# Linear attention and an MLP mixer on one core: token mixing two slots sooner, and another order of phi, transposes and loads

## The chip, the core and the metric

The kernel runs on one core of one Trainium2 chip. The metric is the device time of one execution in microseconds (us); the time before is the median of three runs. Five engines work side by side and wait for one another by semaphores: PE (TensorE, matrix products), DVE (VectorE), ACT (ScalarE), POOL (GpSimd) and SP (SyncE, which here only issues DMAs). Each runs its own instructions strictly in the order in which the program gives them.

## What is computed

```
phi(x) = where(x > 0, x, exp(x) - 1) + 1
kv  = einsum('bhsd,bhse->bhde', phi(k), v);  z = sum_s phi(k)
x   = einsum('bhsd,bhde->bhse', phi(q), kv) / (einsum('bhsd,bhd->bhs', phi(q), z) + 1e-6)
x   = x.transpose(0, 2, 1, 3).reshape(8, 576, 512)
u   = x + (relu(x^T @ w_tok1) @ w_tok2)^T          # token mixing: 576 -> 256 -> 576
out = u + relu(u @ w_ch1) @ w_ch2                  # channel mixing: 512 -> 1536 -> 512
```

q, k and v are float32 of 8 batches, 8 heads, 576 rows and 64 columns; the output is float32. Products are made in bf16 and summed in float32.

## The kernel before, in words

**Tiles.** The 576 rows of a batch are 4 x 128 rows and a tail of 64; the tails of two batches share one tile of 128. `load` (L99) fetches one tensor of one batch for half of the heads with two DMAs of SP: 512 KB (L104) and the tail of 64 KB (L106). The raw tiles have two buffers per tensor, by even and odd batch, so the load of batch n + 2 waits until batch n's raw tile has been read.

**Steps of the attention of one batch.** `phi` makes phi(k) or phi(q) for half of the heads: an exponential on ACT (L116, "e"), then on DVE y = x + 1 (L122), a minimum (L130) and a maximum (L131, into "kp" or "qp"). `vcast` turns v into bf16 (L144 and the tail L145, into "vs" and "vst"). `kv` multiplies (L163) and ACT copies to "kvbd" (L167). phi(q) is transposed to "qT", for the first four batches by PE and a copy of ACT (`qtr`, L173 and L187), for later ones by one crossbar DMA of SP (`qtr_dma`, L191). `nd` makes numerator and denominator on PE (L200) and divides on DVE (L210 to L213, into "x").

**Token mixing.** `mm1` (L235) with a relu on ACT (L238, "ar"), then `mm2` (L246) for the row groups 0 and 1 ("mm2a"), 2 and 3 ("mm2b") and the tail ("mm2t"); DVE adds x and writes u (L252) or the tail's ut (L250). u is transposed to uT: for batches 0 and 1 by PE with copies (`utr`), for later ones by two crossbar DMAs of SP (`utr_dma`, L333); the tail goes to uTt (L338 from batch 3 on).

**Channel mixing.** `mm3` (L349) makes one of 12 blocks of 128 hidden channels from uT with four products of 128 x 512, and ACT applies the relu (L353, "cr"). `mm3_tail` (L360) does the same for the tails of a pair of batches. `mm4` (L372) multiplies by w_ch2 into one of nine output tiles of a pair; DVE adds u (L382, "o_sb"), and POOL (SP for the last pair) stores it. `mm3` and `mm4` share four PSUM banks, the small steps two tiles of two banks each.

**What sets the order.** `run` (L540) writes the order out by hand. The channel mixing of batch n is a row of slots: 12 of `mm3`; for odd n then 3 of `mm3_tail` and 15 of `mm4` (30 slots), for even n 12 of `mm4` (24 slots). Behind each slot come the small steps of the next batch that a table gives this slot number: `at0` in batch 0's loop, `at1` in batch 1's, `AT3` and `AT` later. One slot of four products keeps PE busy for 0.86 us. The phi and the casts of batch n + 2 and its loads stand in the same lists, so all engines' queues follow from these tables. In batch 0's loop, slots 12 to 23 are `m4_0`: one product for each of four output tiles at a time, which need all four banks of `mm3` free.

The DMAs of SP are issued in program order too: a load that waits holds up the transposes behind it, and the other way round. Batch 1's loads come first k, then v, then q; the second part of w_ch2 (POOL, L437) is made to wait for v's second half, and batch 2's first load for the third part of w_ch2.

The functions that the change touches, and what calls them:

Of the kernel before, what the change touches and what calls it, by code (L numbers as in the profile page):

```python
# [18 lines left out]
def kernel(  # L19
# [23 lines left out]
    R = 4  # L43
# [195 lines left out]

    def mm2(n, rs):  # L240
        b = n % 2
        m = len(rs)
        ps = ps_sm.tile([128, 2, DM], FP32, name="h_ps", tag="sm")
        for i, r in enumerate(rs):
            for kt in range(NT):
                nc.tensor.matmul(out=ps[:, i], lhsT=w2t[:, kt, b, :] if r == R else w2v[:, kt, r],  # L246
                                 rhs=ar[b][:, kt, :], start=(kt == 0), stop=(kt == NT - 1))
        if rs[0] == R:
            h = half[b]
            nc.vector.tensor_tensor(out=ut[n // 2 % 2][h], in0=ps[h, 0], in1=x[b][h, R], op=ALU.add)  # L250
        else:
            nc.vector.tensor_tensor(out=u[b][:, rs[0]:rs[0] + m], in0=ps[:, 0:m],  # L252
                                    in1=x[b][:, rs[0]:rs[0] + m], op=ALU.add)
# [173 lines left out]
    NB = 4  # L427
# [92 lines left out]
    def steps(n):  # L520
# [34 lines left out]
    def m4_0(kc):  # L555
        for t in range(R):
# [8 lines left out]
    fill += [(5, lambda: phi("k", 1, 0, HG)), (7, lambda: phi("k", 1, HG, HG)),
             (9, lambda: vcast(1, 0, nc.vector.tensor_copy)),
             (11, lambda: vcast(1, 1, nc.vector.tensor_copy))]
    fill += [(at0[nm], fn) for nm, fn in steps(1) if nm[:2] == "kv"]
    fill += [(12, lambda: phi("q", 1, 0, HG)), (12, lambda: phi("q", 1, HG, HG))]
    fill += [(at0[nm], fn) for nm, fn in steps(1) if nm[:2] in ("qt", "nd", "mm")]  # L570
    fill += [(23, lambda: mm4_end(0, 0))]
# [6 lines left out]
    big = m3(1) + m3t + m4(0, [4, 5, 6, 7, 8])  # L578
    at1 = {"kv0": 10, "kv1": 11, "qt0": 12, "qt1": 13, "nd00": 14, "nd01": 15, "nd10": 16,
           "nd11": 17, "nd20": 18, "nd21": 19, "mm1": 21, "mm2a": 23, "mm2b": 24, "mm2t": 26,  # L580
           "uta": 23, "utb": 24}
    fill = [(s, lambda g=g: prep_k(2, g, nc.vector.tensor_copy)) for g, s in ((0, 2), (1, 4))]
    fill += [(s, lambda g=g: phi("q", 2, HG * g, HG)) for g, s in ((0, 7), (1, 9))]
    fill += [(at1[nm], fn) for nm, fn in steps(2)]
    fill += [(s, lambda g=g: prep_k(3, g)) for g, s in ((0, 20), (1, 22))]
    fill += [(s, lambda g=g: phi("q", 3, HG * g, HG)) for g, s in ((0, 26), (1, 28))]
    fill += [(28, lambda: load_all(4, "qkv"))]
    run(big, sorted(fill, key=lambda e: e[0]))
    load_all(5, "qkv")

    AT3 = {"kv0": 0, "kv1": 1, "qt0": 2, "qt1": 3, "nd00": 4, "nd01": 5, "nd10": 6, "nd11": 7,
           "nd20": 8, "nd21": 9, "mm1": 11, "mm2a": 13, "mm2b": 14, "mm2t": 16, "uta": 13,
           "utb": 14, "utt": 16}
    AT = {"kv0": 0, "kv1": 1, "nd00": 3, "nd01": 4, "nd10": 5, "nd11": 6, "nd20": 7, "nd21": 8,
          "mm1": 10, "mm2a": 12, "mm2b": 13, "mm2t": 15, "uta": 12, "utb": 13, "utt": 15}
    for n in range(2, B):
        p, b = divmod(n, 2)
        if b == 0:
            big = m3(n) + m4(p, [0, 1, 2, 3])
        else:  # L600
            big = m3(n) + m3t + m4(p, [4, 5, 6, 7, 8] if n + 1 < B else [8, 4, 5, 6, 7])
# [41 lines left out]
```

## Time and profile before

| what | value |
|---|---|
| median of 3 runs (lowest to highest) | 287.98 us (287.26 to 289.92) |
| the profiled execution | 288.99 us |
| its span, first to last instruction | 287.2 us |
| PE busy | 264.2 us (92%) |
| DVE, ACT, POOL busy | 165.3, 145.9, 29.2 us |
| mean granted clock of PE | 0.992 |
| moved by DMA | 47.98 MB, mean 167 GB/s |

The profile is one execution. A row of a timeline has the start in us from the span's beginning, the duration (of several merged instructions, if it ends in x4 and the like), the engine, the line of the kernel, the operation, output and inputs, and in square brackets how long the engine stood idle before it and what ended this. A row with an engine's name and a "q" is the issue of a DMA, not its transfer. In the waits, a row gives who waited for whom, the total, how often, and the longest. In the table by stretches, each engine has its busy time and its count; the last three columns are PE's granted clock (1.00 is full), the mean busy share of the DMA engines and the GB/s that they moved.

### The profile page before, as it was taken

The page shows a single profiled execution, that of the slowest core. Times are in us where ns is not written, and L with a number is a line of the kernel's source. Part 1 is how long each engine was busy: PE and PEld are TensorE (multiplying, and loading weights), DVE is VectorE, ACT ScalarE, POOL GpSimd, SP SyncE. Part 2 cuts the span into 40 slices and gives each one's busy share as a digit, 9 for nine tenths or more (in the row PEclk, how much of TensorE's full clock was granted, in tenths as well). Part 3 has the DMA queues.
Part 4 walks back from the last instruction along what each step waited for, and adds up shares of the span by engine and source line. Part 5 has one row for each costly group of instructions (what it writes and reads, how often), then busy time and mean ns, then how long its engine had stood idle before and what let it go on. Part 6 is the DMA issues. An engine that isn't in the chain of part 4 may idle for free.

```text
span 287.2 us, 4625 instructions
## 1 busy us (share of the span) xinstructions
PE 264.2 (92%) x1784; PEld 146.8 (51%) x1804; DVE 165.3 (58%) x327; ACT 145.9 (51%) x233; POOL 29.2 (10%) x52
## 2 busy tenths in 40 slices
PE   8798978979999789897999999998999999999993
PEld 8776444544754345343556455444565454444641
DVE  4885276767877925767476718593858444520021
ACT  3664776038974337770677335943577065106400
POOL 3090020003000210002000220011000210000000
PEclk9999999999999979999999999999999999999999
DMA  6979999999701799999974994096009310340031
GB/s 209 280 109 198 281 271 177 290 282 341 220 21 52 129 276 311 289 229 267 288 211 92 252 351 150 2 192 138 2 0 189 123 37 0 69 137 34 2 110 73
DMA packets 70901, 47.98 MB, mean 167 GB/s; under 512 B 39328, under 2 KB 67872, under 8 KB 70880
## 3 DMA queue, kind: packets, MB, share of 16 engines
q1 hardware_dynamic: 64384, 36.84, 51.8%
q0 software_dynamic: 6496, 10.85, 15.7%
q8 instruction: 14, 0.23, 0.3%
q14 instruction: 7, 0.06, 0.1%
HBM read 35.85 MB, written 9.44 MB: 158 GB/s over the span
## 4 chain that ended last, share of the span: by engine, by line
PE 65%; DMA 14%; ACT 6%; SPq 5%; DVE 5%; issue 3%; POOL 1%; ACTq 0%
PE h_ps L372 25%; PE c_ps L349 23%; DMA uT<-u 6%; DMA q_raw<-in_q_dram 6%; PE a_ps L235 5%; PE h_ps L246 4%; DMA wc<-in_moe_w_ch_dram 3%; PE c_ps L360 3%; PE nd_ps L200 3%; SPq L106 3%; ACT e L116 2%; PE kv_ps L163 2%; SPq L104 2%; DVE u L252 1%; ACT cr L353 1%
## 5 line engine op out<-in xcount | busy, mean ns | idle before, releaser
L349 PE MATMUL c_ps<-uT,wc 128*128 128x512 bf16 x384 | 93.0, 382 | 7.1 <-DMA uT<-u 6.3
L353 ACT ACTIVATE cr<-c_ps 128x512 bf16<-128x512 f32 x96 | 56.3, 600 | 78.3 <-PE c_ps L349 78.3
L372 PE MATMUL h_ps<-wc,cr 128*128 128x512 bf16 x375 | 88.0, 379 | 0.8 <-DMA wc<-in_moe_w_ch_dram 0.3
L372 PEld LDWEIGHTS <-cr 128*128 128x128 bf16 x384 | 36.9, 98 | 41.6 <-issue 0.4
L349 PEld LDWEIGHTS <-wc 128*128 128x128 bf16 x384 | 35.8, 98 | 43.1 <-DMA uT<-u 5.8
L382 DVE TENSOR_TENSOR o_sb<-h_ps,u 128x512 f32<-128x512 f32 x32 | 21.5, 686 | 18.7 <-PE h_ps L372 18.7
L386 POOL DMA_DIRECT2D out_dram<-o_sb x24 | 14.4, 601 | 162.4 <-DVE o_sb L382 145.1
L213 DVE TENSOR_TENSOR x<-nd_ps,den 128x512 bf16<-128x512 f32 (+1 forms) x48 | 28.9, 603 | 1.7
L210 DVE TENSOR_SCALAR den<-nd_ps 128x8 f32<-128x8 f32 (+1 forms) x48 | 7.8, 162 | 33.7 <-PE nd_ps L200 33.2
L130 DVE TENSOR_SCALAR e<-e 128x1280 bf16<-128x1280 bf16 (+1 forms) x34 | 16.0, 471 | 14.7 <-ACT e L116 14.7
L252 DVE TENSOR_TENSOR u<-h_ps,x 128x1024 bf16<-128x1024 f32 x14 | 16.6, 1219 | 12.5 <-PE h_ps L246 12.5
L116 ACT ACTIVATE e<-k_raw 128x1280 bf16<-128x1280 f32 x16 | 20.4, 1273 | 4.2 <-DMA k_raw<-in_k_dram 4.1
L116 ACT ACTIVATE e<-q_raw 128x1280 bf16<-128x1280 f32 (+1 forms) x18 | 20.5, 1156 | 2.7 <-DMA q_raw<-in_q_dram 1.9
L200 PEld LDWEIGHTS <-qT 128*128 128x128 bf16 x160 | 12.6, 98 | 11.3 <-ACT qT L187 0.7
L200 PE MATMUL nd_ps<-kvbd,qT 128*128 128x130 bf16 x160 | 16.8, 221 | 0.7 <-ACT kvbd L167 0.5
L238 ACT ACTIVATE ar<-a_ps 128x512 bf16<-128x512 f32 x14 | 7.6, 594 | 19.2 <-PE a_ps L235 19.2
L122 DVE TENSOR_SCALAR y<-k_raw 128x1280 bf16<-128x1280 f32 x16 | 13.1, 821 | 4.7 <-DMA k_raw<-in_k_dram 4.5
L405 PE MATMUL bank<-identity 128*128 128x128 bf16 x178 | 13.6, 244 | 1.4 <-POOL identity masks.py:199 1.4
L246 PE MATMUL h_ps<-ar,w 128*128 128x512 bf16 x53 | 14.2, 379 | 0.2
L235 PE MATMUL a_ps<-x,w 128*128 128x512 bf16 x50 | 14.1, 379 | 0.3
L122 DVE TENSOR_SCALAR y<-q_raw 128x1280 bf16<-128x1280 f32 x16 | 13.2, 825 | 1.8 <-DMA q_raw<-in_q_dram 1.5
L131 DVE TENSOR_TENSOR qp<-e,y 128x1280 bf16<-128x1280 bf16 (+1 forms) x18 | 13.5, 752 | 0.6
(86 smaller groups left out, 238.2 us busy)
## 6 DMA issues: line engine op xcount, KB each, us to landing
k_raw<-in_k_dram SPq DMA_DIRECT2D x16, 512.0 KB, 7.5
q_raw<-in_q_dram SPq DMA_DIRECT2D x16, 512.0 KB, 7.4
v_raw<-in_v_dram SPq DMA_DIRECT2D x16, 512.0 KB, 8.1
out_dram<-o_sb POOLq DMA_DIRECT2D x24, 256.0 KB, 4.3
wc<-in_moe_w_ch_dram POOLq DMA_DIRECT2D x8, 384.0 KB, 8.2
out_dram<-o_sb SPq DMA_DIRECT2D x8, 256.0 KB, 2.5
k_raw<-in_k_dram SPq DMA_DIRECT2D x16, 64.0 KB, 7.1
q_raw<-in_q_dram SPq DMA_DIRECT2D x16, 64.0 KB, 6.9
```

Source lines behind the costliest of these rows:

```text
L116: nc.scalar.activation(out=e, in_=f, func=AF.Exp)
L122: nc.vector.tensor_scalar(out=y, in0=f, scalar1=1.0, scalar2=None, op0=ALU.add)
L130: nc.vector.tensor_scalar(out=e, in0=e, scalar1=1.0, scalar2=None, op0=ALU.min)
L200: nc.tensor.matmul(out=ps[:, i, a * 2 * D1:(a + 1) * 2 * D1], lhsT=qT[b][:, r, j, :], rhs=kvbd[b][:, j, :], start=True, stop=True)
L213: nc.vector.tensor_tensor(out=x[b][:, rs[0]:rs[0] + m, HG * D * g:HG * D * (g + 1)].rearrange("p r (h d) -> p r h d", h=HG), in0=v_[:, :, ...
L235: nc.tensor.matmul(out=ps[:, mt], lhsT=w1t[:, b, ms] if r == R else w1[:, r, ms], rhs=x[b][:, r, :], start=(r == 0), stop=(r == R))
L246: nc.tensor.matmul(out=ps[:, i], lhsT=w2t[:, kt, b, :] if r == R else w2v[:, kt, r], rhs=ar[b][:, kt, :], start=(kt == 0), stop=(kt == NT ...
L252: nc.vector.tensor_tensor(out=u[b][:, rs[0]:rs[0] + m], in0=ps[:, 0:m], in1=x[b][:, rs[0]:rs[0] + m], op=ALU.add)
L349: nc.tensor.matmul(out=ps, lhsT=wc1[:, kj, 128 * mc:128 * mc + 128], rhs=uT[b][:, :, kj], start=(kj == 0), stop=(kj == NDM - 1))
L353: nc.scalar.activation(out=cr[b][:, mc, :], in_=ps, func=AF.Relu)
L372: nc.tensor.matmul(out=ps, lhsT=crt[:, kc, :] if t == 8 else cr[b][:, kc, 128 * r:128 * r + 128], rhs=wc2[:, kc, :], start=(kc == 0), stop ...
L382: nc.vector.tensor_tensor(out=o, in0=ps, in1=ut[p % 2] if t == 8 else u[b][:, r, :], op=ALU.add)
```

## The change

- In batch 0's loop the loads of batch 1 come in the order k, q, v, and the second part of w_ch2 waits for q's second half. phi q goes to slots 9 and 11, its transposes to 12 and 13, and v's casts and both kv products behind them to 14 (before: casts 9 and 11, kv 11, phi q 12, transposes 14 and 15). nd and mm1 move one slot forward, mm1 from 22 to 21; mm2 stays at 23.
- For batch 1 alone `mm2` of the row groups 2 and 3 adds x on PE, by two more products with the identity, and ACT copies the result to u; for the row groups 0 and 1 DVE adds as before.
- In batch 1's loop phi k of batch 2 moves from slots 2 and 4 to 0 and 2, without v's casts, which come at 4 (now on ACT) and 5 (DVE); phi q from 7 and 9 to 6 and 8; kv from 10 and 11 to 7 and 8; the transposes, nd and mm1 one slot forward (mm1 from 21 to 20), mm2a and mm2b and the transposes of u from 23 and 24 to 21 and 22, the tail from 26 to 24. phi k and the casts of batch 3 go from 20 and 22 to 19 and 23, phi q from 26 and 28 to 25 and 27. Batches 4 and 5 are loaded at slots 24, 25 and 28, in the order k, v, q, where batch 4 was loaded at slot 28 and batch 5 behind the loop, each q, k, v.
- From batch 2's loop on nd, mm1, mm2 and the transposes of u stand one slot sooner, both kv products in slot 0. phi q of batch n + 2 moves from slots 9 and 11 to 8 and 9 (9 and 10 in batch 2's loop), phi k with the casts from 17 and 19 to 14 and 16 (15 and 17). qT's crossbar transpose goes from slot 11, ahead of u's, to slot 12 (13), behind u's. The loads of batch n + 4 come together at slot 18 (before: q at 15, k and v at 20).

The diff, cut to its core (the tables' rows are told above):

```diff
-    def mm2(n, rs):
+    def mm2(n, rs, add=False):
...
                 nc.tensor.matmul(out=ps[:, i], lhsT=w2t[:, kt, b, :] if r == R else w2v[:, kt, r],
-                                 rhs=ar[b][:, kt, :], start=(kt == 0), stop=(kt == NT - 1))
+                                 rhs=ar[b][:, kt, :], start=(kt == 0),
+                                 stop=(kt == NT - 1 and not add))
+            if add:
+                nc.tensor.matmul(out=ps[:, i], lhsT=identity, rhs=x[b][:, r, :], start=False,
+                                 stop=True)
...
+        elif add:
+            nc.scalar.copy(out=u[b][:, rs[0]:rs[0] + m], in_=ps[:, 0:m])
...
     for g in range(2):
+        landed["q1", g] = load("q", 1, g)
+    for g in range(2):
         landed["v1", g] = load("v", 1, g)
-    for g in range(2):
-        landed["q1", g] = load("q", 1, g)
-    c2_in += [after(load_wc2(i), landed["v1", 1] if i == 1 else None) for i in range(1, NB)]
+    c2_in += [after(load_wc2(i), landed["q1", 1] if i == 1 else None) for i in range(1, NB)]
...
-                 ("mm2b", lambda: mm2(n, [2, 3])), ("mm2t", lambda: mm2(n, [R]))]
+                 ("mm2b", lambda: mm2(n, [2, 3], n == 1)), ("mm2t", lambda: mm2(n, [R]))]
...
-           "uta": 23, "utb": 24}
-    fill = [(s, lambda g=g: prep_k(2, g, nc.vector.tensor_copy)) for g, s in ((0, 2), (1, 4))]
+           "uta": 21, "utb": 22}
+    fill = [(s, lambda g=g: phi("k", 2, HG * g, HG)) for g, s in ((0, 0), (1, 2))]
+    fill += [(4, lambda: vcast(2, 0)), (5, lambda: vcast(2, 1, nc.vector.tensor_copy))]
...
-            fill += [(15, lambda: load_all(n + 4, "q"))]
-            for g, s in ((0, 17), (1, 19)):
-                fill += [(s, lambda g=g: prep_k(n + 2, g))]
-            fill += [(20, lambda: load_all(n + 4, "kv"))]
+            d = 1 if n == 2 else 0
+            fill += [(s + d, lambda g=g: phi("q", n + 2, HG * g, HG)) for g, s in ((0, 8), (1, 9))]
+            fill += [(12 + d, lambda: qtr_dma(n + 2))]
+            fill += [(s + d, lambda g=g: prep_k(n + 2, g)) for g, s in ((0, 14), (1, 16))]
+            fill += [(18, lambda: load_all(n + 4, "kvq"))]
```

Three places show what this does to the order of an engine. The lines of the changed kernel are seven higher from `mm2` on (L252 becomes L259). The number behind a name is its buffer: k_raw_78, q_raw_82, x_93 and u_97 belong to odd batches, k_raw_77, q_raw_81, x_92 and u_96 to even ones. A row may stand for several instructions (x2).

ACT in batch 0's loop, from the eighth block of `mm3` on. Before:

```order
L353 ACTIVATE cr_103<-c_ps 128x512 x2
L116 ACTIVATE e<-k_raw_78 128x1280
L353 ACTIVATE cr_103<-c_ps 128x512 x4
L167 CAST kvbd_91<-kv_ps 64x2x65 x4
L116 ACTIVATE e<-q_raw_82 128x1280 x2
L187 COPY qT_89<-tp 128x2x5x128 x2
L238 ACTIVATE ar_95<-a_ps 128x512 x2
```

Now:

```order
L360 ACTIVATE cr_103<-c_ps 128x512 x2
L116 ACTIVATE e<-k_raw_78 128x1280
L360 ACTIVATE cr_103<-c_ps 128x512 x2
L116 ACTIVATE e<-q_raw_82 128x1280
L360 ACTIVATE cr_103<-c_ps 128x512 x2
L116 ACTIVATE e<-q_raw_82 128x1280
L187 COPY qT_89<-tp 128x2x5x128 x2
L167 CAST kvbd_91<-kv_ps 64x2x65 x4
L238 ACTIVATE ar_95<-a_ps 128x512 x2
```

The first exponential of phi q has moved ahead of the last two relus, and the copies of kv behind those of qT.

DVE in batch 1's loop, behind the last x of batch 2. Before:

```order
L382 TENSOR_TENSOR o_sb<-h_ps,u_97 128x512
L122 TENSOR_SCALAR y<-k_raw_78 128x1280
L130 TENSOR_SCALAR e<-e 128x1280
L131 TENSOR_TENSOR kp<-e,y 128x4x5x64
L122 TENSOR_SCALAR y<-k_raw_78 128x1280
L130 TENSOR_SCALAR e<-e 128x1280
L131 TENSOR_TENSOR kp<-e,y 128x4x5x64
L382 TENSOR_TENSOR o_sb<-h_ps,u_97 128x512
L252 TENSOR_TENSOR u_96<-h_ps,x_92 128x1024 x2
```

Now:

```order
L122 TENSOR_SCALAR y<-k_raw_78 128x1280
L130 TENSOR_SCALAR e<-e 128x1280
L131 TENSOR_TENSOR kp<-e,y 128x4x5x64
L389 TENSOR_TENSOR o_sb<-h_ps,u_97 128x512
L259 TENSOR_TENSOR u_96<-h_ps,x_92 128x1024 x2
L389 TENSOR_TENSOR o_sb<-h_ps,u_97 128x512
L122 TENSOR_SCALAR y<-k_raw_78 128x1280
L130 TENSOR_SCALAR e<-e 128x1280
L131 TENSOR_TENSOR kp<-e,y 128x4x5x64
```

Both writes of u stand between the halves of phi k now, where they stood behind both.

SP at the end of the burst of loads, in batch 2's loop. Before:

```order
L104 DMA v_raw_80<-in_v_dram 128x4x256
L106 DMA v_raw_80<-in_v_dram 64x4x64
L191 DMA_TRANSPOSE qT_88<-qp 128x20x128
L333 DMA_TRANSPOSE uT_101<-u_97 128x8x128 x2
L104 DMA q_raw_81<-in_q_dram 128x4x256
```

Now:

```order
L104 DMA q_raw_82<-in_q_dram 128x4x256
L106 DMA q_raw_82<-in_q_dram 64x4x64
L340 DMA_TRANSPOSE uT_101<-u_97 128x8x128 x2
L191 DMA_TRANSPOSE qT_88<-qp 128x20x128
L345 DMA_TRANSPOSE uTt<-ut_99 128x4x128
L104 DMA k_raw_77<-in_k_dram 128x4x256
```

u's transposes stand directly behind the loads and ahead of q's, and all three transposes ahead of batch 6's first load.

More of the change, by code (lines that the diff above doesn't have):

```diff
@@ L560 @@
         [lambda kc=kc: m4_0(kc) for kc in range(NCH)]
-    at0 = {"kv0": 11, "kv1": 11, "qt0": 14, "qt1": 15, "nd00": 16, "nd01": 17, "nd10": 18,
-           "nd11": 19, "nd20": 20, "nd21": 21, "mm1": 22, "mm2a": 23, "mm2b": 23, "mm2t": 23,
+    at0 = {"qt0": 12, "qt1": 13, "kv0": 14, "kv1": 14, "nd00": 15, "nd01": 16, "nd10": 17,
+           "nd11": 18, "nd20": 19, "nd21": 20, "mm1": 21, "mm2a": 23, "mm2b": 23, "mm2t": 23,
            "ut": 23, "utt": 23}
@@ L565 @@
     fill += [(5, lambda: phi("k", 1, 0, HG)), (7, lambda: phi("k", 1, HG, HG)),
[L566 to L570, printed above, removed]
+             (9, lambda: phi("q", 1, 0, HG)), (11, lambda: phi("q", 1, HG, HG))]
+    fill += [(14, lambda g=g: vcast(1, g, nc.vector.tensor_copy)) for g in range(2)]
+    fill += [(at0[nm], fn) for nm, fn in steps(1) if nm[:2] in ("kv", "qt", "nd", "mm")]
     fill += [(23, lambda: mm4_end(0, 0))]
@@ L602 @@
         fill = []
-        if n + 2 < B:
-            fill += [(s, lambda g=g: phi("q", n + 2, HG * g, HG)) for g, s in ((0, 9), (1, 11))]
-            fill += [(11, lambda: qtr_dma(n + 2))]
         if n + 1 < B:
```

24 lines of the change are left out of this document (12 added, 12 removed).

## The prediction

> **What bounds the kernel now.** I read the busy shares first, then TensorE's waits, its timeline at each wait, and there the timelines of the engine or queue that ended the wait.
>
> ```profile
> PE 264.2 (92%) x1784; PEld 146.8 (51%) x1804; DVE 165.3 (58%) x327; ACT 145.9 (51%) x233; POOL 29.2 (10%) x52
> PE c_ps L349 <- DMA uT<-u: 6.3, 3, 3.2
> ```
>
> TensorE (PE) is the bound: 264.2 of 287.2 us. So a change can only take the 23 us in which PE stands, or the stretch in which it runs at a lower clock. The longest wait of the big loops is for uT, the crossbar transpose of u (6.3 us in 3 waits). Here are these waits in PE's timeline, with one that DVE ends, and then rows of the table by stretches of time.
>
> ```profile
> 101.93 1.89 PE L349 MATMUL c_ps<-uT,wc 128*128 128x512 bf16 x4 [3.19 <-DMA uT<-u]
> 106.46 1.03 PE L349 MATMUL c_ps<-uT,wc 128*128 128x512 bf16 x4
> 119.66 0.38 PE L235 MATMUL a_ps<-x,w1t 128*128 128x512 bf16 x1 [1.27 <-DVE x L213]
> 135.33 1.02 PE L349 MATMUL c_ps<-uT,wc 128*128 128x512 bf16 x4 [1.70 <-DMA uT<-u]
> 138.19 1.89 PE L349 MATMUL c_ps<-uT,wc 128*128 128x512 bf16 x8
> 196.78 1.02 PE L349 MATMUL c_ps<-uT,wc 128*128 128x512 bf16 x4 [1.37 <-DMA uT<-u]
> ...
> 102.00:104.00 2.00, 2.00 (x8) 0.90 (x9) 0.32 (x1) 0.09 (x1) 1.07 (x2) 0.50 0.98 297
> 104.00:106.00 2.00, 2.00 (x15) 1.30 (x13) 0.00 (x0) 1.03 (x3) 0.00 (x0) 0.66 0.97 275
> 133.00:136.00 3.00, 1.30 (x7) 0.44 (x6) 1.50 (x3) 0.00 (x0) 1.08 (x2) 1.00 1.15 248
> ```
>
> The reader is to see two prices of one wait. After the 3.19 us the granted clock is 0.50 and then 0.66 (third column from the right); after the 1.70 us it stays 1.00. Two channel steps with both kv products take 138.19 - 135.33 = 2.86 us at full clock, but 106.46 - 101.93 = 4.53 us behind the long wait: 1.67 us more. The wait at 101.93 thus costs 4.86 us. With 1.27, 1.70 and 1.37 that is 9.2 us behind us 98.
>
> Durations come from one execution of 288.99 us (span 287.2, so 1.79 lies around it), 1.01 above the median of 287.98. I take the sum off the median.
>
> **Part by part. Batch 1's loop (us 64 to 102).** The mixing of batch 2 moves two slots forward, and the second half of phi k of batch 3 goes behind u. From the timelines of DVE, PE, ACT and SP:
>
> ```profile
> 92.18 0.49 DVE L130 TENSOR_SCALAR e<-e 128x1280 bf16<-128x1280 bf16 x1 [1.80 <-ACT e L116]
> 94.05 2.35 DVE L252 TENSOR_TENSOR u<-h_ps,x 128x1024 bf16<-128x1024 f32 x2
> ...
> 92.96 1.03 PE L246 MATMUL h_ps<-ar,w 128*128 128x512 bf16 x4
> ...
> 89.77 1.09 ACT L238 ACTIVATE ar<-a_ps 128x512 bf16<-128x512 f32 x2 [5.66 <-PE a_ps L235]
> 95.98 2.75 PE L372 MATMUL h_ps<-wc,crt 128*128 128x512 bf16 x12
> ...
> 95.30 3.64 SPq L333 DMA_TRANSPOSE uT<-u  x2
> 99.03 1.34 SPq L104 DMA_DIRECT2D q_raw<-in_q_dram  x1
> ```
>
> Before, DVE stood 1.80 us for phi k's exponential and only then made u, ending at 96.40; the batch's products end at about 98.73 and uT is there 5.53 us after u. After: a slot is four products, 0.86 us, so the second product ends at 93.99 - 1.73 = 92.27. Only one slot now lies between mm1 and mm2, less than the 1.09 us of ar, so PE waits some 0.35 us: 92.6. With 0.2 us to start and 1.22 for the last u (row of 2.35 for two) u ends at 94.0, 2.4 us sooner. PE ends at 99.1, uT is there at 99.5.
>
> But ACT gets more to do early in this loop: the cast of v's first half moves to it from DVE, and the exponentials come sooner, ahead of cr tiles. From ACT's timeline, and PE's one wait for it:
>
> ```profile
> 82.59 1.08 ACT L144 CAST vs<-v_raw 128x1024 bf16<-128x1024 f32 x1
> 83.70 0.41 ACT L145 CAST vst<-v_raw 64x256 bf16<-64x256 f32 x1
> 67.16 0.60 ACT L353 ACTIVATE cr<-c_ps 128x512 bf16<-128x512 f32 x1 [0.27 <-PE c_ps L349]
> 78.25 1.22 ACT L187 COPY qT<-tp 128x1280 bf16<-128x1280 bf16 x1
> ...
> 81.14 0.40 PE L200 MATMUL nd_ps<-kvbd,qT 128*128 128x130 bf16 x4 [0.23 <-ACT qT L187]
> ```
>
> 1.08 + 0.41 come to about 1.35 us overlapped. ACT was nearly full from 65 to 81; of its gaps there (the 0.27 shown and two like it just before) 0.8 us can be used up. Walking the new order with these durations, kv0 waits for the cast, the second q transposes for phi, and nd for both qT copies: about 1.4 us of PE waits for 0.23 before and some slots won; I take 0.75 us lost, between 0 (kv comes three slots sooner and gives slack) and 2.0 (all of the cast and of a delayed exponential). PE and u slip together, so the stage gains 101.93 - 99.5 - 0.75 = 1.7, and 1.9 with a little from the transposes, whose first now runs 1.7 us ahead of the second. The remaining wait of about 0.4 is far under 3.19, so the 1.67 us of slow clock go too. **Sum 3.6.**
>
> **Batch 2's loop.** phi q of batch 4 stood on DVE ahead of the last x; that is where 1.27 came from. Now both halves stand behind all x and ahead of u: **1.27 gained**, and u is delayed by phi for 1.3 us, which the rest of the loop covers. At the loop's end the SP queue counts (its timeline, with the rows of DVE and PE that it is measured against):
>
> ```profile
> 120.73 1.13 SPq L106 DMA_DIRECT2D v_raw<-in_v_dram  x1
> 121.97 6.73 SPq L191 DMA_TRANSPOSE qT<-qp  x1
> 128.80 2.81 SPq L333 DMA_TRANSPOSE uT<-u  x2
> ...
> 153.65 2.95 SPq L191 DMA_TRANSPOSE qT<-qp  x1
> ...
> 125.48 1.22 DVE L252 TENSOR_TENSOR u<-h_ps,x 128x1024 bf16<-128x1024 f32 x1
> ...
> 127.42 6.21 PE L372 MATMUL h_ps<-wc,cr 128*128 128x512 bf16 x27
> ...
> DMA to landing us min/median/max: 3.0/4.5/5.8
> ```
>
> u was there at 126.7, yet uT was issued at 128.80 behind qT, which itself stood 6.73 us behind the burst of loads (2.95 where none are ahead). Now uT stands in front of qT: 2.95 sooner; and the loads begin when batch 2's u is through, 1.65 sooner (2.4 - 0.75): 124.2. The last row (uT's DMAs) gives 3.0 to 5.8 to landing; I take 5.3, in its upper half, since loads are still ahead: 129.5. PE arrives after 28.76 us of loop (127.42 + 6.21 - 101.93, less 1.67 and 1.27) behind a start at 100.0: 128.8. A wait of 0.7 stays of 1.70: **1.0 gained** (0 to 1.7). Behind uT waits qT now, some 3 us later, 132.5; nd of the next loop wants it after three slots and the kv products, 129.5 + 2.6 + 1.1 = 133.2: just hidden, and each us that uT is later beyond that is paid by PE.
>
> The Trainium skill, "DMA: Bandwidth & Descriptors", Queues, rings and completion order, says that a DMA engine takes one queue's descriptors in ring order. That speaks against the change: a burst issued at once must drain before uT. The 6.73 us agree.
>
> **Batch 4's loop.** No loads are in the way there:
>
> ```profile
> 186.10 2.35 DVE L252 TENSOR_TENSOR u<-h_ps,x 128x1024 bf16<-128x1024 f32 x2
> 186.24 3.11 SPq L191 DMA_TRANSPOSE qT<-qp  x1
> 189.45 3.55 SPq L333 DMA_TRANSPOSE uT<-u  x2
> ```
>
> With qT's 3.11 behind it, uT lands some 3 us sooner and PE would have needed only 1.37: **1.37 gained**. The loops of batches 3 and 5 (30 slots) wait for nothing now; their gain is nothing. That k, v and q are loaded together at slot 18 costs nothing: they are used a loop later, some 30 us, and stand behind every transpose of their own loop. Nor do both kv products in slot 0: kp and vs are made in the loop before.
>
> **Batch 0's loop (us 26 to 64).** q lands where v did, so phi q fills the time before kv. From the timelines again:
>
> ```profile
> 38.05 2.06 ACT L353 ACTIVATE cr<-c_ps 128x512 bf16<-128x512 f32 x4
> 40.21 0.40 PE L163 MATMUL kv_ps<-vs,kp 128*128 128x130 bf16 x4 [1.36 <-DVE vs L144]
> 45.80 0.73 PE L173 MATMUL tp<-identity,qp 128*128 128x128 bf16 x10 [1.06 <-DVE qp L131]
> 46.85 1.02 PE L372 MATMUL h_ps<-wc,cr 128*128 128x512 bf16 x4 [0.32 <-DMA wc<-in_moe_w_ch_dram]
> 43.09 1.27 ACT L116 ACTIVATE e<-q_raw 128x1280 bf16<-128x1280 f32 x1 [0.35 <-DMA q_raw<-in_q_dram]
> 41.09 2.24 POOL L437 DMA_DIRECT2D wc<-in_moe_w_ch_dram  x3 [19.39 <-DMA v_raw<-in_v_dram]
> 58.71 2.14 PE L246 MATMUL h_ps<-ar,w 128*128 128x512 bf16 x7
> 60.03 2.35 DVE L252 TENSOR_TENSOR u<-h_ps,x 128x1024 bf16<-128x1024 f32 x2 [4.17 <-PE h_ps L246]
> ```
>
> Waits of 1.36 and 1.06 seem to be the prize, but most return: an exponential of 1.27 now stands ahead of two cr, so the four banks that the output products need are free at 41.4 rather than 40.1; and wc2's second part still lands at 46.85, as its gate is the load in the same place. By then PE has done one more set of transposes than before: 0.57 us. mm1 a slot sooner takes away 0.4 of waiting for ar (58.71 took 2.14 for 1.73 of products). u's second half goes to ACT beside DVE, 1.2 us side by side, for two more products of 0.43 and the ACT copy's longer chain: 0.2. **Sum 1.1** (-1 to 1.8).
>
> Total: 1.1 + 1.9 + 1.67 + 1.27 + 1.0 + 1.37 = 8.3 us; 287.98 - 8.3 = **279.7 us**.
>
> **Rivals.** *ACT sets batch 1's loop* (2.0 lost instead of 0.75), uT of batch 2 comes 0.5 later and the 1.0 at batch 2's end is not won: 279.7 + 1.25 + 0.5 + 1.0 = 282.5. For it: the full ACT rows; against it: kv's three slots of slack.
>
> *The median run has no slow clock to lose.* The runs of before lie at 287.26 to 289.92, the profiled one 1.01 above the median; if the median run does not pay the 1.67, they cannot be won: 281.4. For it: that spread is as wide as the price. Against it: the wait of 3.19 comes from the order, which is the same in every run. The Trainium skill, "TensorE: Matmul & The Clock Gate", Part 1, bears on this: the clock falls after an idle window of about 3.4 us whose start runs freely, so a wait of 3.19 would meet it in some runs alone; the trace shows one run, in which it fell.
>
> *uT is no sooner*, the change not doing what it says: DMA takes what u won, since loads follow directly. Then 3.6 falls to -0.75 and 1.0 to 0: 1.1 + 1.27 + 1.37 - 0.75 = 3.0, 285.0. Against it: loads stand behind uT in the queue.
>
> *q late in batch 0's loop*: if q lands at 43.09 as now, ACT stops at its exponential with two cr behind it and PE starts its output products at 45.4 instead of 41.7, with a wait long enough for the slow clock: 279.7 + 3.7 + 1.7 = 285.1. Against it: v1, in that place, had landed by 41.09 (POOL's row).
>
> *The burst holds uT of batch 3*: slower. Twelve pairs of loads stand ahead of it; their sizes and the rates of two stretches:
>
> ```profile
> k_raw<-in_k_dram SPq DMA_DIRECT2D x16, 512.0 KB, 7.5
> k_raw<-in_k_dram SPq DMA_DIRECT2D x16, 64.0 KB, 7.1
> 98.00:102.00 4.00, 0.81 (x5) 0.20 (x4) 3.90 (x7) 0.00 (x0) 0.44 (x1) 0.99 0.84 188
> 124.00:126.00 2.00, 2.00 (x11) 1.00 (x10) 2.00 (x3) 2.00 (x4) 0.14 (x1) 1.00 1.14 287
> ```
>
> 7.1 MB from us 98: at the 287 GB/s of most of the burst they end at 123, at the 188 of the stretch beside transposes at 135.6. uT would land 4.5 later (the median above), 11.3 us after PE's arrival and with the slow clock again: 287.98 - 7.3 won elsewhere + (11.3 - 1.7) + 1.7 = 292.0. The change is slower from a wait of 7.3 us on, that is with the burst under about 210 GB/s. Against it: the burst has 275 at us 104 and 287 at 124.
>
> **How the numbers follow.** Forecast 0.55 (own range 277.2 to 281.7: batch 1's loss 0 to 2.0, batch 0's gain -1 to 1.8, batch 2's 0 to 1.7, not all at one end), no slow clock 0.13, ACT 0.15, uT no sooner 0.06, q late 0.06, burst 0.05. The range of 277.0 to 284.3 takes in the first three and leaves out the last three. One per cent, 2.9 us, is about what a measurement here can tell from no change: faster (under 285.1) takes the first three and, as they end at 285.0 and 285.1, half of the next two, 0.89 and a little less for what I do not see: 0.88; same 0.07; slower 0.05.
>
> **What would show it.** PE's wait before batch 2's first channel product under 1 us and no granted clock under 0.9 behind us 90; no wait for x in batch 2's loop; uT ahead of qT and under 1 us of waiting at the ends of batches 2 and 4; in batch 0's loop output products from about 41.4. I am wrong if PE's waits between 70 and 82 pass 2 us, or uT's wait moves to batch 2's end and grows.

## The result, and the profile after

| | before | after |
|---|---|---|
| median of 4 runs each (lowest to highest) | 288.52 us (287.26 to 289.92) | 279.2 us (278.03 to 279.61) |
| ratio, 95% interval | | 0.967 (0.961 to 0.973) |
| profiled execution, span | 288.99 us, 287.2 us | 279.19 us, 277.4 us |

The change makes the kernel 3.3% faster; 279.7 had been predicted. Disturbed runs are left out of the ratios but not of the medians below, and the profiled executions of experiments 1 and 4 are such runs, 3.1 and 2.8 us above their kernels' medians, so I read their waits for their place and not for their size.

First the busy times of the changed kernel, then from its timeline of PE the first product of the channel mixing of batches 1 to 5, each the start of that batch's loop:

```profile
PE 262.3 (95%) x1786; PEld 146.3 (53%) x1806; DVE 164.6 (59%) x324; ACT 147.6 (53%) x236; POOL 28.6 (10%) x52
```

```profile
63.15 3.19 PE L356 MATMUL c_ps<-uT,wc 128*128 128x512 bf16 x14
98.40 1.03 PE L356 MATMUL c_ps<-uT,wc 128*128 128x512 bf16 x4
126.84 1.03 PE L356 MATMUL c_ps<-uT,wc 128*128 128x512 bf16 x4
159.64 1.03 PE L356 MATMUL c_ps<-uT,wc 128*128 128x512 bf16 x4
186.97 1.03 PE L356 MATMUL c_ps<-uT,wc 128*128 128x512 bf16 x4
```

None of these rows has a bracket: PE no longer waits for uT at any of them. PE does 1.9 us less of busy time with two products more, which fits the end of the slow stretch. Of the starts before, the prediction shows those of batches 2, 3 and 5; these are the ones of batches 1 and 4, from PE's timeline before:

```profile
64.37 1.89 PE L349 MATMUL c_ps<-uT,wc 128*128 128x512 bf16 x8
167.92 1.03 PE L349 MATMUL c_ps<-uT,wc 128*128 128x512 bf16 x4
```

The difference of two starts is the length of a loop, and tells where the time came from. Batch 0's loop starts at 26.37 before and 26.53 after.

| loop of batch | before, us | after, us | won | predicted |
|---|---|---|---|---|
| 0 | 38.00 | 36.62 | 1.4 | 1.1 |
| 1 | 37.56 | 35.25 | 2.3 | 1.9 |
| 2 | 33.40 | 28.44 | 5.0 | 1.67 + 1.27 + 1.0 = 3.9 |
| 3 | 32.59 | 32.80 | -0.2 | 0 |
| 4 | 28.86 | 27.33 | 1.5 | 1.37 |
| 5 to 7 | 90.46 | 90.45 | 0 | 0 |

In the stretches around and behind the long wait the granted clock was 0.99, 0.50 and 0.66 before (third column from the right). The table by stretches of the changed kernel has full clock there:

```profile
98.00:102.00 4.00, 4.00 (x42) 2.73 (x41) 3.72 (x6) 2.16 (x6) 0.56 (x1) 1.00 1.10 330
102.00:104.00 2.00, 2.00 (x18) 1.24 (x17) 0.00 (x0) 2.00 (x4) 1.07 (x2) 1.00 1.14 350
104.00:106.00 2.00, 2.00 (x17) 1.14 (x15) 1.36 (x5) 1.96 (x3) 0.00 (x0) 1.00 1.07 348
```

SP's queue around batch 2's end in the changed kernel (the prediction shows it before), and then the view of the tile uT there: when its two transposes were issued, and how long each took to land.

```profile
118.45 4.88 SPq L340 DMA_TRANSPOSE uT<-u  x2
123.43 3.59 SPq L191 DMA_TRANSPOSE qT<-qp  x1
```

```profile
L340 SPq DMA_TRANSPOSE uT<-u x2: 1872/2396/2921, 118.4 to 121.5; - x2
DMA to landing us min/median/max: 4.6/5.8/7.0
```

Counted from the loop's start, uT was issued 128.80 - 101.93 = 26.87 us in before, and 118.45 - 98.40 = 20.05 after. That is the place where qT stood (121.97 - 101.93 = 20.04). The second transpose, issued at 121.5, lands 4.6 us later, at 126.1; PE needs it at 126.84.

### The profile page after: what moved, and what is told of

Read it like the earlier page. It is cut to its first block, busy times and chain, and to the rows that moved or that the text cites. A ratio compares the mean times of both kernels' runs of the same rounds, so it can differ in the third digit from the quotient of the medians.

```text
span 277.4 us, 4607 instructions
## 1 busy us (share of the span) xinstructions
PE 262.3 (95%) x1786; PEld 146.3 (53%) x1806; DVE 164.6 (59%) x324; ACT 147.6 (53%) x236; POOL 28.6 (10%) x52
## 4 chain that ended last, share of the span: by engine, by line
PE 78%; DMA 9%; ACT 4%; DVE 3%; SPq 2%; issue 1%; POOL 1%; ACTq 0%; DVEq 0%
PE h_ps L379 33%; PE c_ps L356 25%; PE a_ps L235 5%; PE h_ps L247 5%; DMA wc<-in_moe_w_ch_dram 3%; PE nd_ps L200 3%; DMA q_raw<-in_q_dram 3%; PE kv_ps L163 3%; PE c_ps L367 3%; DMA k_raw<-in_k_dram 3%; SPq L106 1%; SPq L104 1%; DVE y L122 1%; ACT e L116 1%; ACT qT L187 1%
## 5 line engine op out<-in xcount | busy, mean ns | idle before, releaser
L360 ACT ACTIVATE cr<-c_ps 128x512 bf16<-128x512 f32 x96 | 56.0, 598 | 70.1 <-PE c_ps L356 70.0
L356 PE MATMUL c_ps<-uT,wc 128*128 128x512 bf16 x384 | 91.3, 379 | 0.8 <-ACT uT L328 0.7
L379 PE MATMUL h_ps<-wc,cr 128*128 128x512 bf16 x377 | 87.7, 379 | 1.9 <-ACT cr L360 1.3
L379 PEld LDWEIGHTS <-cr 128*128 128x128 bf16 x384 | 37.0, 98 | 43.5 <-issue 1.9
L356 PEld LDWEIGHTS <-wc 128*128 128x128 bf16 x384 | 35.9, 98 | 36.5 <-issue 1.2
L393 POOL DMA_DIRECT2D out_dram<-o_sb x24 | 13.8, 574 | 155.1 <-DVE o_sb L389 136.5
L259 DVE TENSOR_TENSOR u<-h_ps,x 128x1024 bf16<-128x1024 f32 x13 | 15.5, 1219 | 13.4 <-PE h_ps L247 13.4
L144 ACT CAST vs<-v_raw 128x1024 bf16<-128x1024 f32 x13 | 13.8, 1063 | 0.1
```

The lines of the kernel that those rows point to most:

```text
L356: nc.tensor.matmul(out=ps, lhsT=wc1[:, kj, 128 * mc:128 * mc + 128], rhs=uT[b][:, :, kj], start=(kj == 0), stop=(kj == NDM - 1))
L360: nc.scalar.activation(out=cr[b][:, mc, :], in_=ps, func=AF.Relu)
L379: nc.tensor.matmul(out=ps, lhsT=crt[:, kc, :] if t == 8 else cr[b][:, kc, 128 * r:128 * r + 128], rhs=wc2[:, kc, :], start=(kc == 0), stop ...
```

## The experiments

The first three each make one part of the change alone, on the kernel before.

**1. Batch 0's part.** q loaded ahead of v, phi q and its transposes ahead of kv, x added on PE for batch 1.

```diff
-    at0 = {"kv0": 11, "kv1": 11, "qt0": 14, "qt1": 15, "nd00": 16, ...
+    at0 = {"qt0": 12, "qt1": 13, "kv0": 14, "kv1": 14, "nd00": 15, ...
...
```

> The kernel before with batch 0's part of the change alone: loads k q v, phi q ahead of kv, u of batch 1 half on ACT. Theory (each part takes away waits of its own, and the parts add up): batch 0's loop 1.2 to 1.4 us shorter, all later loops as before, so about 287.2 against 288.5. Rival (the loads set the pace, so what PE wins it gives back at its next wait): PE's wait for uT at the end of batch 1's loop grows by as much, time unchanged.

Measured: 286.37 us, ratio 0.994 (0.991 to 0.997). By the ratio that is 1.7 us (0.8 to 2.7) of 288.48, so the gain is there, and the 1.1 of the forecast lies within its interval. The rival, under which the time would not change, falls. The size is hard to pin down, since this loop is not the same length in every execution: 38.0, 37.05 and 37.07 us in the three profiles with the old order (before, experiments 2 and 3); 36.15 to 36.62 in nine and 37.6 in two of the eleven with the new one. By the medians of these loops it wins 0.7 us.

**2. Batch 1's loop.** The table `at1`, phi k's second half behind u, and the loads of batches 4 and 5 in a burst.

```diff
-            "nd11": 17, "nd20": 18, "nd21": 19, "mm1": 21, "mm2a": 23, "mm2b": 24, "mm2t": 26,
+            "nd11": 16, "nd20": 17, "nd21": 18, "mm1": 20, "mm2a": 21, "mm2b": 22, "mm2t": 24,
...
```

> The kernel before with batch 1's loop of the change alone (phi k sooner, v's first cast on ACT, mixing two slots sooner, loads of batches 4 and 5 sooner). Theory: the wait for uT of 3.19 us goes, PE loses some 0.5 to 0.8 us to ACT, the slow clock behind the wait (1.67 us) goes: 4.0 us, and the earlier loads take up to 1 us off the wait at the end of batch 2's loop: 283.5 to 284.5. Rival (the slow clock is no part of the usual run, or the transposes only land as late because loads follow): 2.3 us or less, 286.2 or more.

Measured: 286.52 us, ratio 0.989 (0.984 to 0.995). By the ratio it wins some 3 us (1.4 to 4.7), between the theory's 4.0 and the rival's 2.3, so the time alone doesn't decide. The trace does: the profiled execution took 284.31 us, with all of PE's waits behind us 85 in its timeline being these, and with full clock from 98 on:

```profile
115.41 0.38 PE L235 MATMUL a_ps<-x,w1t 128*128 128x512 bf16 x1 [1.27 <-DVE x L213]
130.79 1.02 PE L349 MATMUL c_ps<-uT,wc 128*128 128x512 bf16 x4 [1.41 <-DMA uT<-u]
192.10 1.02 PE L349 MATMUL c_ps<-uT,wc 128*128 128x512 bf16 x4 [1.23 <-DMA uT<-u]
```

The wait at batch 1's end is gone, so this part alone ends it, and the slow clock with it; the waits for x and at the ends of batches 2 and 4 stay, as they belong to the next part.

**3. From batch 2's loop on.**

```diff
-            fill += [(11, lambda: qtr_dma(n + 2))]
+            fill += [(12 + d, lambda: qtr_dma(n + 2))]
```

(with the tables `AT3` and `AT`, phi and the loads as in the change)

> The kernel before with the change from batch 2's loop on alone (phi q behind all x, u's transposes ahead of q's, mixing one slot sooner, loads together). Theory: the wait for x (1.27) goes, the waits for uT at the ends of batch 2's and batch 4's loops (1.70 and 1.37) go, less what the loads, which start as late as before, leave of the first: 3.0 to 4.3 us, 284.2 to 285.5. Rival (the burst of loads holds uT of batch 3 wherever it stands): 2.6 us or less.

Measured: 285.21 us, ratio 0.988 (0.984 to 0.993). One wait behind us 85 is left in PE's timeline, with its slow clock in the stretch behind it:

```profile
102.03 1.89 PE L349 MATMUL c_ps<-uT,wc 128*128 128x512 bf16 x4 [4.21 <-DMA uT<-u]
```

```profile
102.00:104.00 2.00, 1.97 (x7) 0.87 (x8) 0.00 (x0) 0.00 (x0) 0.77 (x2) 0.50 1.00 280
```

Waits for x and for uT at the ends of batches 2 and 4 are gone, as expected. The wait that is left is 1.0 us longer than before, although nothing ahead of it was changed: uT took up to 6.1 us to land here and 5.1 before. So a landing alone can differ by about 1 us between two executions. The three ratios multiply to 0.972; the whole change has 0.967.

**4. qT ahead of u again**, the rest as in the changed kernel.

```diff
-            fill += [(12 + d, lambda: qtr_dma(n + 2))]
+            fill += [(10 + d, lambda: qtr_dma(n + 2))]
```

> The changed kernel with q's crossbar transpose ahead of u's again, all else as changed. Theory (the place in the queue counts where loads are still under way): uT of batch 3 comes about 3 us later, PE waits 1 to 2 us at the end of batch 2's loop, nothing at the end of batch 4's, where some 4 us are to spare, and the 0.2 us for qT at the start of batch 3's loop goes: 280.0 to 281.0 against 279.2. Rival (u being sooner is enough): no new wait, 279.2 or less.

Measured: 287.44 us, ratio to before 0.993 (0.988 to 0.997). Both expectations are missed by far: putting this one row of SP's queue back loses 0.993 - 0.967 = 0.026, or some 7 of the 9.5 us that the change brings. PE's timeline, SP's, and the landing of uT:

```profile
135.15 1.86 PE L356 MATMUL c_ps<-uT,wc 128*128 128x512 bf16 x4 [8.76 <-DMA uT<-u]
```

```profile
119.20 5.33 SPq L191 DMA_TRANSPOSE qT<-qp  x1
124.62 5.57 SPq L340 DMA_TRANSPOSE uT<-u  x2
```

```profile
DMA to landing us min/median/max: 8.1/8.1/8.1
```

uT is issued 6 us later than in the changed kernel and then takes 8.1 us to land. Around that time POOL issues the stores of batch 2's four output tiles (256 KB each); these are the last three:

```profile
123.41 0.55 POOL L393 DMA_DIRECT2D out_dram<-o_sb  x1 [3.00 <-DVE o_sb L389]
126.01 0.54 POOL L393 DMA_DIRECT2D out_dram<-o_sb  x1 [2.05 <-DVE o_sb L389]
127.42 0.54 POOL L393 DMA_DIRECT2D out_dram<-o_sb  x1 [0.86 <-DVE o_sb L389]
```

That made the next theory: transposes slow down beside stores. It would also explain why the same order cost only 1.70 us of waiting in the kernel before. There uT was issued as far into the loop (26.87 us; here 124.62 - 97.79 = 26.83) and landed within 5.5 us, but the last three stores came later, the last two when uT was about to land:

```profile
129.48 0.55 POOL L386 DMA_DIRECT2D out_dram<-o_sb  x1 [3.05 <-DVE o_sb L382]
134.20 1.14 POOL L386 DMA_DIRECT2D out_dram<-o_sb  x2 [4.17 <-DVE o_sb L382]
```

So the 7 us are not what this order cost before. They are what the change would have lost if it had kept the order.

**5. The same without batch 2's four stores.** That part of the output is not written.

```diff
+        if p == 1 and t < R:
+            return
```

> The kernel after the change with q's crossbar transpose ahead of u's again, and with the stores of batch 2's four output tiles left out (that part of the output is missing). Tells apart why qT ahead of uT cost a wait of 8.76 us at the end of batch 2's loop. Theory (transposes slow down beside the output stores; in the changed kernel uT passes before they start): the wait falls from 8.8 to 1 to 2 us, clock stays up, 280 to 281 us. Rival (qT's own place in the queue costs this much, whatever else the DMA engines move): the wait stays 7 to 8 us, 286 to 287.5 us.

Measured: 281.28 us, ratio 0.978 (0.973 to 0.983). The theory holds. PE's wait and uT's landing:

```profile
128.58 1.02 PE L356 MATMUL c_ps<-uT,wc 128*128 128x512 bf16 x4 [1.37 <-DMA uT<-u]
```

```profile
DMA to landing us min/median/max: 3.3/3.3/3.3
```

uT is issued at 123.79, nearly as late as in experiment 4, and lands in 3.3 instead of 8.1 us. By the ratios, of the 0.026 that qT ahead costs against the changed kernel, 0.011 (some 3 us) are its place in the queue and 0.015 (some 4 us) the stores with the slow clock behind the longer wait, as far as leaving them out wins nothing else. Each of these ratios is known to about 0.005.

**6. phi q ahead of the last x in batch 2's loop**, as before.

```diff
-            fill += [(s + d, lambda g=g: phi("q", n + 2, HG * g, HG)) for g, s in ((0, 8), (1, 9))]
+            if n == 2:
+                fill = [(8, lambda: phi("q", n + 2, 0, HG))] + fill + [(10, ...
```

> The kernel after the change with the first half of phi q of batch 4 ahead of batch 2's last x on DVE, as it was before. Theory of the prediction (1.27 us of waiting for x were won by taking phi q out of the way, and nothing gives them back): a wait of 1.0 to 1.4 us for x before the token mixing of batch 3, the stage of batch 2 longer by as much, 280.2 to 280.6 us. Rival (the slots in between absorb it): wait under 0.4, 279.0 to 279.5 us.

Measured: 280.73 us, ratio 0.975 (0.969 to 0.980), whose interval overlaps that of the changed kernel, so it is the trace that shows the price. The wait is back to the hundredth, and the loop is 29.87 us long instead of 28.44:

```profile
113.93 0.38 PE L235 MATMUL a_ps<-x,w1t 128*128 128x512 bf16 x1 [1.27 <-DVE x L213]
```

**7. Mixing and transposes one slot later from batch 2's loop on, order kept.**

```diff
-           "nd20": 7, "nd21": 8, "mm1": 10, "mm2a": 12, "mm2b": 13, "mm2t": 15, "uta": 12,
+           "nd20": 7, "nd21": 8, "mm1": 11, "mm2a": 13, "mm2b": 14, "mm2t": 16, "uta": 13,
...
```

> The kernel after the change with token mixing, u's and q's transposes one slot later from batch 2's loop on, their order kept. Theory (the order of qT and uT and the 24.9 us start of the loads do the work, and uT has a slack of some 1.5 us at batch 2's end, so a slot of 0.86 us is covered): wait for uT at the ends of batches 2 and 4 under 0.4 us, 279.0 to 279.8 us. Rival (the slot itself is what was won, since a later uT meets the output stores, beside which a transpose takes about four times as long): waits of 2 us or more at batch 2's end, 281 to 283 us.

Measured: 279.53 us, ratio 0.972 (0.966 to 0.978).

```profile
126.89 1.02 PE L356 MATMUL c_ps<-uT,wc 128*128 128x512 bf16 x4 [0.76 <-DVE o_sb L389]
```

The total is as the theory had it, but a wait of 0.76 stands at batch 2's end, where I had counted on a slack of 1.5. The row names DVE's o_sb; yet uT's second transpose, issued at 121.3, took 5.5 us to land, at 126.8, so it was uT. The slack of the changed kernel is 126.84 - 126.1 = 0.7 us. There is none to spare at batch 2's end, but no cliff behind it either: at batch 4's end the slot costs nothing. So the order is worth some 7 us here (experiment 4), and the slot under one.

**8. phi k's second half ahead of u in batch 1's loop.**

```diff
-    fill += [(s, lambda g=g: prep_k(3, g)) for g, s in ((0, 19), (1, 23))]
+    fill += [(s, lambda g=g: prep_k(3, g)) for g, s in ((0, 19), (1, 20))]
```

> The kernel after the change with the second half of phi k of batch 3 ahead of u again in batch 1's loop. Tells how much of the end of the wait at 101.93 is the order on DVE and how much the two slots. Theory (DVE stands 0.5 to 1.8 us for the exponential, u comes some 1.2 us later, and uT's slack is about 1.0): wait before batch 2's first channel product 0 to 0.6 us, full clock, 279.2 to 279.9 us. Rival (this order was most of the 3.19 us, and the two slots little): wait of 2 us or more, 281 to 283 us, the more if the clock falls.

Measured: 282.61 us, ratio 0.982 (0.975 to 0.988). The time lies in the rival's range, but the wait does not: it is 1.39 us, between the two expectations, and a second wait adds to the time that neither had.

```profile
101.46 1.04 PE L356 MATMUL c_ps<-uT,wc 128*128 128x512 bf16 x4 [1.39 <-DMA uT<-u]
132.19 1.02 PE L356 MATMUL c_ps<-uT,wc 128*128 128x512 bf16 x4 [2.11 <-DMA uT<-u]
```

```profile
92.33 0.49 DVE L130 TENSOR_SCALAR e<-e 128x1280 bf16<-128x1280 bf16 x1 [1.72 <-ACT e L116]
```

DVE stands 1.72 us for the exponential, u comes that much later and PE waits 1.39 of it. So the order on DVE accounts for 1.4 of the 3.19, and the rest of that part of the change, the two slots among it, for 1.8. The second wait, 2.11 at batch 2's end, needed an experiment of its own.

**9. Experiment 8 with the four loads of batch 5's q behind u's and q's transposes.**

```diff
-             (28, lambda: load_all(5, "q"))]
...
+            if n == 2:
+                fill.append((13, lambda: load_all(5, "q")))
```

> The kernel of the run before with phi k of batch 3 ahead of u, but with the four loads of batch 5's q issued behind u's and q's transposes instead of ahead of them. There, PE waited 1.39 us for uT at batch 1's end and 2.11 at batch 2's end, where the change alone has no wait; u of batch 3 was made at 121.5 and uT issued at 123.13, when the loads had been issued. Theory (the burst, begun 0.9 us later against the loop, set the second wait: four loads take 4.3 us of SP's time): the first wait stays at 1.2 to 1.6, the second falls under 0.7, 280.3 to 281.5 us. Rival (u itself is late there, or uT meets the output stores): the second wait stays at 1.5 or more, 282 to 283 us.

Measured: 281.06 us, ratio 0.978 (0.974 to 0.981). PE's timeline from 60 to 140 holds a uT wait only at batch 1's end. Here it is, and then SP's row at batch 2's end in experiment 8 and in this one:

```profile
100.09 1.04 PE L356 MATMUL c_ps<-uT,wc 128*128 128x512 bf16 x4 [1.44 <-DMA uT<-u]
```

```profile
123.13 5.30 SPq L340 DMA_TRANSPOSE uT<-u  x2
```

```profile
120.15 2.66 SPq L340 DMA_TRANSPOSE uT<-u  x2
```

The theory holds: the second wait was the burst of loads, which stood ahead of uT in SP's queue. With four loads fewer ahead, uT issues in 2.66 us where it took 5.30, and batch 2's loop is 28.45 us long.

**10. The changed kernel again**, beside 9 and 11.

> The kernel after the change, unchanged, beside the two others of this call: 278.8 to 279.9 us, its stages as in its first profile within 0.1 us from batch 1's loop on; batch 0's loop may differ by up to 1 us, as it did between three runs of one and the same code for that loop (38.0, 37.1 and 37.1 us).

Measured: 279.48 us, ratio 0.970 (0.967 to 0.973). Its loops: 36.15, 35.26, 28.44, 32.59, 27.32 us. The 0.2 that batch 3's loop had lost in the first profile is not there.

**11. First token product of batch 2 at slot 19, all of v's casts on DVE.**

```diff
-            "nd11": 16, "nd20": 17, "nd21": 18, "mm1": 20, "mm2a": 21, ...
+            "nd11": 16, "nd20": 17, "nd21": 18, "mm1": 19, "mm2a": 21, ...
...
-    fill += [(4, lambda: vcast(2, 0)), ...
+    fill += [(4, lambda: vcast(2, 0, nc.vector.tensor_copy)), ...
```

> The kernel after the change with batch 2's first token product one slot sooner (slot 19) and all casts of v of batch 2 on DVE instead of half on ACT. Theory (PE waits some 0.4 us for ar between the two products, and the cast on ACT costs 0.3 to 0.6 in batch 1's loop): batch 1's loop 34.4 to 34.9 us instead of 35.25, 278.3 to 278.9 us. Rival (the cast only moves the wait to DVE, which makes u): batch 1's loop 35.1 us or more, 279.2 us or more.

Measured: 280.49 us, ratio 0.976 (0.971 to 0.980); batch 1's loop 36.30 us. The rival's time and length of loop come out, but by another way than the cast: DVE first, then PE, then uT's landing at batch 1's end:

```profile
88.24 0.49 DVE L130 TENSOR_SCALAR e<-e 128x1280 bf16<-128x1280 bf16 x1 [3.37 <-ACT e L116]
```

```profile
98.98 1.04 PE L356 MATMUL c_ps<-uT,wc 128*128 128x512 bf16 x4 [2.32 <-DMA uT<-u]
```

```profile
DMA to landing us min/median/max: 4.9/5.5/6.1
```

The loop starts at 62.68, so PE arrived 1.3 us sooner into it (98.98 - 2.32 - 62.68 = 33.98 instead of 35.25), with no wait for qp or qT left in its timeline there, but u did not come sooner: the relu of ar now stood ahead of phi k's exponential on ACT, and DVE waited for that with u behind it. uT then took up to 6.1 us to land against 4.6 in the changed kernel; why, was not settled (experiment 3 has a difference of 1.0 without a cause in the program). Part of the median's loss is the clock's: the three runs with a mean clock of 0.988 to 0.994 took 281.4 to 282.7 us, the other three, at 0.997 to 1.0, 279.3 to 279.6. All casts on DVE together with the order of the next experiment was not tried.

**12. The same slot with the exponential kept ahead**, casts as in the change.

```diff
-            ... "mm1": 20, "mm2a": 21, ...
+            ... "mm1": 19, "mm2a": 21, ...
-    fill += [(s, lambda g=g: prep_k(3, g)) for g, s in ((0, 19), (1, 23))]
+    fill += [(s, lambda g=g: prep_k(3, g)) for g, s in ((0, 18), (1, 23))]
```

> The kernel after the change with batch 2's first token product at slot 19 instead of 20 and the first half of phi k of batch 3 at slot 18 instead of 19, so that its exponential stays ahead of the relu of ar on ACT (in the run before, where it fell behind, DVE stood 3.37 us for it and u came no sooner). Theory (PE's 0.4 us of waiting for ar go, u is made that much sooner since DVE waits 2.02 us for PE there, and uT with it): batch 1's loop 34.7 to 34.9 us instead of 35.25, nothing lost behind it, 278.6 to 279.1 us. Rival (uT, which lands some 0.4 us ahead of PE, doesn't follow, and PE waits for it): batch 1's loop 35.1 us or more, 279.2 us or more.

Measured: 279.77 us, ratio 0.971 (0.969 to 0.973); batch 1's loop 35.00 us, with no wait for uT behind it. The wait for ar was 0.25 us and not 0.4, and that is what the loop won. It is too little for the medians (279.77 against 279.48 for the changed kernel) to show; no version here is measurably faster than the change.

## Why the prediction was right, and where its steps were off

The sign, the mechanism and the sum came out. Two sizes inside did not.

- **PE is the bound, and the waits and the slow clock are what can be won.** Right: all four waits behind us 98 are gone, and 9.2 was their price; the loops of batches 1, 2 and 4 won 8.8.
- **Batch 1's loop, 1.9.** It won 2.3, and experiment 2 has the same length of loop alone (35.27). Against 3.19 of wait removed, 0.9 was lost in the loop, which is what my terms give (0.35 for ar and 0.75 for ACT, less 0.2). Of it 0.6 has a name: PE waits 0.25 for qp, 0.32 for qT and 0.25 for ar, where it waited 0.23 before. The 0.4 of wait for uT that I expected to stay did not: uT, issued at 93.4 and landing 4.6 us later, is there 0.4 us ahead of PE.
- **The slow clock, 1.67.** Right in its size, but not as a fixed consequence of the wait. In the traces' records of the granted clock, a stretch at 0.50 lasts 3.41 us or two or three times that (3.41 from us 101.95 before, 6.83 in experiment 3, 10.24 in experiment 4). The shortest one thus costs half of 3.41, or 1.7 us, and 0.006 of the mean clock: the profiles with none have a mean of 0.997 to 1.0, those with one of 0.991 to 0.993. All 43 runs of the kernel before that enter the ratios of the experiments lie at 0.978 to 0.994, in two groups: 21 at 0.990 to 0.994 (286.2 to 288.2 us) and 22 at 0.978 to 0.988 (287.8 to 289.8 us). Of ten runs of the changed kernel, eight lie at 0.997 to 1.0 and two at 0.993. So every run before paid for at least one slow stretch, and half of them for more; the rival of a median run with no slow clock to lose falls. The mean does not say where the stretch was. In experiments 1, 2, 6 and 10 one stands between us 11 and 16, and one run of experiment 3, which keeps the long wait, has a mean of 0.997 and so did not pay for it.
- **x, 1.27.** Right to the hundredth by the traces of experiment 6 and of the change.
- **uT at batch 2's end, 1.0 with 0.7 of wait staying. This step failed in its size**, at "2.95 sooner". I had read the 6.73 us of qT's issue as time lost to the loads, with 2.95 as qT's own share. But uT did not get 2.95 of it back: it took over qT's whole place, 6.82 us sooner in the loop (26.87 against 20.05). It gave 1.1 of this back, since it now stands behind the loads itself (landing at 27.7 us into the loop instead of 33.4, 5.7 sooner; by my terms 3.9). The term for the landing was off the other way: 5.3 us from issue, where 7.65 passed. So the whole 1.70 was won, and a slack of 0.7 us besides. Of the 5.0 that batch 2's loop won, 1.67 + 1.27 + 1.70 = 4.6 have a name; 0.3 have not.
- **qT, just hidden.** Right, with nothing to spare: batch 3's loop lost 0.2 in one profile and nothing in the other.
- **Batch 4's end, 1.37.** It won 1.5.
- **Batch 0's loop, 1.1.** Between 0.7 and 1.4. The output products start at 40.89 behind a wait of 1.27 us for cr, near the 41.4 of the forecast.

  ```profile
  40.89 0.86 PE L379 MATMUL h_ps<-wc,cr 128*128 128x512 bf16 x2 [1.27 <-ACT cr L360]
  ```

- **The rivals.** ACT did not set batch 1's loop, but it is near: in experiment 11 one relu ahead of one exponential is enough. uT was sooner, issued 91.65 - 63.15 = 28.5 us into batch 1's loop instead of 95.30 - 64.37 = 30.9; and q was not late, as the output products start at 40.89 and not at 45.4 (that rival counts from 41.7, where the rest of the prediction has 41.4). The burst did not hold uT of batch 3, though it is nearer to deciding than its 0.05 suggested: experiment 8 delayed it against the loop by less than a microsecond and lost 2.11 us, and experiment 9 took four loads out and had them back. The Trainium skill, "DMA: Bandwidth & Descriptors", Queues, rings and completion order, has it that a DMA engine serves a queue's descriptors in ring order; the runs fit this, as uT's issue took 5.30 us behind all the loads and 2.66 with four fewer ahead. The rate alone did not decide, and the bound of 210 GB/s was too low: the burst moved a mean of 300 GB/s in the changed kernel (us 94.7 to 118.3), and 286 in experiment 8 (us 98.6 to 123.0), where it cost 2.11 us. My 4.5 us from the last load to uT's landing were the term that was off; in experiment 8 PE could start 132.19 - 123.13 = 9.1 us after uT's issue. In the changed kernel SP had issued the last load at 118.23, 0.2 us ahead of uT.

## What to carry to other kernels

Where transposes, loads and stores are under way at the same time, the place in the queue of the one transfer that the bound engine waits for can be worth more than the duration of the transfer that it overtakes (6.82 us against 2.95 here): price a swap by the whole delay of the place that it leaves and takes, and ask what starts to run beside it if it comes late. Look then for the slack behind each wait that was removed (0.4 and 0.7 us here, less than the 1.0 by which one landing differed between two executions), since the next edit spends it. And a step is sooner only if every queue that feeds it is: a product moved a slot ahead won 0.25 us in experiment 12, and lost 1.0 in the profile of experiment 11, where an exponential had slipped behind it.

## What was not expected of the hardware

- A crossbar transpose beside stores is far slower than without them. uT lands in 3.3 us without the four stores (experiment 5) and in 8.1 with them (experiment 4), for the same tile issued at nearly the same time; the ratios, 0.978 and 0.993, go the same way. Counted in the trace's list of DMA packets, transposes move 1106 packets of 256 B per us from 124.5 to 127 of the changed kernel, where no store's packet is in flight, and 310 from 125 to 129 of experiment 4, beside the stores' packets of 4 KB. That the stores are the cause is shown by their removal; how the two hinder each other is not.
- The granted clock does not fall right when PE stops, and the length of PE's wait does not settle whether it falls. In experiment 4, where PE stood 8.76 us from 126.4 on, the stretches show it:

  ```profile
  128.00:130.00 2.00, 0.00 (x0) 0.00 (x0) 0.00 (x0) 0.00 (x0) 0.00 (x0) 1.00 1.25 245
  130.00:132.00 2.00, 0.00 (x0) 0.00 (x0) 0.00 (x0) 0.00 (x0) 0.00 (x0) 0.62 1.18 296
  132.00:134.00 2.00, 0.00 (x0) 0.00 (x0) 0.00 (x0) 0.00 (x0) 0.00 (x0) 0.50 1.05 224
  ```

  It is full for some 4 us, then halves. Waits of 3.19 and 4.21 us (before, experiment 3) were followed by 0.50; those of 2.32 and 2.11 (experiments 11 and 8) by 1.00. But in experiment 1 four products behind a wait of 3.25 took 1.04 us, at full clock, and four behind a wait of 2.28 took 1.87, at half:

  ```profile
  102.38 1.04 PE L356 MATMUL c_ps<-uT,wc 128*128 128x512 bf16 x4 [3.25 <-DMA uT<-u]
  134.71 1.87 PE L356 MATMUL c_ps<-uT,wc 128*128 128x512 bf16 x4 [2.28 <-DMA uT<-u]
  ```

  In experiment 8 a wait of only 1.32 us, in batch 0's loop, was followed by 3.41 us at 0.50 from us 42.9 on. So these runs give no length of wait above which the clock falls. The Trainium skill, "TensorE: Matmul & The Clock Gate", Part 1, gives an idle window of about 3.4 us whose start runs freely. The slow stretches of 3.41, 6.83 and 10.24 us fit such a window in their lengths, and the 4.21 us of waiting, the 2.32 and the 2.11 agree with it. The falls behind 3.19, 2.28 and 1.32 us do not, since so short a wait holds no whole window; by that rule a wait of 3.19 would be followed by the slow clock in no run, and not in some, as the prediction has it. Here the measurement decides, and what makes the clock fall stays open.
